# Attention with a mixture layer on one core: local probabilities transposed by a DMA from a float16 pair in SBUF

## Chip, cores, metric

The kernel runs on one core of a Trainium2 chip (trn2). The metric is the device time of one execution in microseconds; before the change the median of three runs is 1051.26 us (1050.98 to 1051.85).

## What is computed

Two attentions over the same q, k, v are added, and the sum goes through a gated layer:

```python
batch, n_heads, seq, head_dim = (8, 8, 576, 64)
q_d, k_d, v_d = means of q, k, v over 4 neighbours      # 144 rows
out_up = repeat(softmax(scale * q_d @ k_d.T) @ v_d, 4)
mask = abs(pos[:, None] - pos[None, :]) < 4
out_local = softmax(where(mask, scale * q @ k.T, -1e9)) @ v
x = (out_up + out_local)                                # 4608 x 512
gate = 1 / (1 + exp(-(x @ w_gate))); val = x @ w_val    # 512 x 1536
return (gate * val) @ w_out                             # 1536 x 512
```

All arrays are float32.

## The kernel before

**Units.** The 64 pairs of batch and head are worked in 32 units of two heads; four units make a batch of 576 tokens. The local attention of a unit is cut into ten blocks of 58 queries, each with its window of 64 keys. Their scores and probabilities lie in one tile `t` of 128 x 640 f32: two blocks share the 128 partitions, five such pairs lie side by side.

**Steps of a unit.** `unit_steps` returns them by name. `s0` and `s1` make the scores (`s_local`, line 475) and `s1` also the exponentials; `sm` (`p2b`, line 500) divides by the sums, for most units on GpSimd, line 507. `a0` and `a1` (`t_local`, line 559) transpose `t`, three blocks of 128 x 128 and then two, on TensorE against the identity into a PSUM tile `at` (line 563), and `parts_of` (line 554) takes it to SBUF as `at16`. For units 0 to 5 (`plain`, NPLAIN = 6) that is one f32 tile. For units 6 to 31 it is a pair of float16 tiles: ScalarE casts the high part (line 555), VectorE subtracts it from the f32 value for the low part (line 557). `x` (`av_local`, line 590) multiplies `at16` with the values `vblk`: ten blocks of three products each (high with high, high with low, low with high; `product`, line 416), then adds the down-sampled output `od` (line 607) and takes the sum apart for the next layer. `d0`, `d1`, `dn`, `at`, `od` do the down-sampled attention with its own small transposes (`adt`, line 573).

**Pools.** `wk` holds `t` and `at16` with two buffers each. PSUM has five banks `mm` and three banks `att`; from unit 4 on the tiles of scores, of both transposes and of `od` share the three.

**The gated layer.** Batches 0 and 1 multiply directly (`moe_gate`, `moe_val`). From batch 2 on `pair` works on two 2x2 blocks at once in seven products (tiles `pg_b_p_..` and `pv_b_p_..`) whose sums VectorE, ScalarE and GpSimd make (lines 811 to 825); twelve pairs a batch, then `act` and `low` leave the product of gate and value as a float16 pair in `gq` (lines 848 and 853). Their weights come from DRAM through a ring of three slots (`wring`, line 782). Then `out_group` and `out_evict` multiply by the output weights: tiles `po_b_m_h`, evicted at lines 729 and 731, stored at line 733.

**Order of the work.** A table of step positions `T` says where each step of each unit stands (`at`, line 886); the units of a batch are worked while the batch before it is in the gated layer. `add` collects the steps, and they are issued in the order of their positions; a scheduler then sets the order on each engine. All DMAs are issued from SP, in order: an issue that waits holds back those behind it.

Of the kernel before, what the change touches and what calls it, by code (L numbers as in the profile page):

```python
# [9 lines left out]
F16 = mybir.dt.float16  # L10
# [9 lines left out]
P = 128  # L20
# [5 lines left out]
R = 58  # L26
WIN = 64
NBLK = 10
NJ = NBLK // 2
# [16 lines left out]
NPLAIN = 6  # L46
# [18 lines left out]
def attention_moe(ctx, tc, qk, qkd, v, vd, wg, wv, wo, mask, out):  # L65
    nc = tc.nc
# [369 lines left out]
    def unit_steps(u):  # L436
# [120 lines left out]
                nc.vector.tensor_tensor(out=dst[1], in0=src, in1=dst[0], op=ALU.subtract)  # L557

        def t_local(j0, j1):
            n = j1 - j0  # L560
            pt = att(f"at_{u}_{j0}")
            for j in range(j0, j1):
                nc.tensor.transpose(pt[:, (j - j0) * P : (j - j0 + 1) * P], s["t"][:, j, :], ident)  # L563
            if j0 == 0:
                s["at"] = in_parts(wk.tile([P, 2, NBLK, R], F16, tag="at", name=f"at16_{u}"), NBLK)
            parts_of([x[:, 2 * j0 : 2 * j1, :] for x in s["at"]], pt[:, : n * P].rearrange("p (g r) -> p g r", r=64)[:, :, :R])

        def t_down():
            mine(ad, u)
# [20 lines left out]
        def av_local(i0, i1):  # L590
            mine(VT, u)
            pt = mm(f"x_{u}_{i0}")
            for i in range(i0, i1):
                product(pt[:, (i - i0) * R : (i - i0 + 1) * R], [x[:, i] for x in VBp], [x[:, i] for x in s["at"]])
            if i0 == 0:
                s["xs"] = xs2 if b >= 2 and u % 2 else xs1
                assert b < 2 or all(("a", k, i) in done for k in "gvo" for i in range(NPC))
                own(s["xs"], u)
            t0, t1 = i0 * R, min(i1 * R, S)
            g0, g1 = t0 // 4, t1 // 4  # L600
            o = s["xs"][:, t0:t1].rearrange("p (g f) -> p g f", f=4)
            x = pt[:, : t1 - t0].rearrange("p (g f) -> p g f", f=4)
            y = s["od"][:, g0:g1].unsqueeze(2).to_broadcast([P, g1 - g0, 4])
            if NPAIR <= u < NPLAIN:
                nc.vector.scalar_tensor_tensor(out=o, in0=x, scalar=sxb[:, b : b + 1], in1=y, op0=ALU.mult, op1=ALU.add)
            else:
                nc.vector.tensor_tensor(out=o, in0=x, in1=y, op=ALU.add)
# [276 lines left out]
        return T["O0"] + T["OD"] * m if b == 0 else start(b) + (TP * (84 + 10.5 * m) / 126 if b < 2 else TB * (72 + 11 * m) / 116)  # L884

    def at(u, k):
        b, hp = divmod(u, NPAIR)
        if b == 0:
            return T[f"p{u}{k}"]
        if b == 1:  # L890
            return T[f"b{u}"] + T["q" + k]
        return start(b) + T[f"m{hp}{k}"] * span(b - 1) / 118
# [178 lines left out]
```

## Time and profile before

| | |
|---|---|
| median of three runs | 1051.26 us (1050.98 to 1051.85) |
| span of the profiled execution | 1051.7 us |
| TensorE | 1018.7 us busy, 97% |
| VectorE | 747.2 us, 71% |
| GpSimd | 556.4 us, 53% |
| ScalarE | 475.6 us, 45% |
| DMA queue of SP | 45.6% of 16 engines, 167.5 MB |

The span of the profiled execution is the time from its first to its last instruction; the profile gives no other time for this execution, and 1051.7 lies inside the spread of the three runs. In the rows further down PE is TensorE, PEld its weight loads, DVE VectorE, ACT ScalarE, POOL GpSimd, SPq SP's queue. A timeline merges neighbouring instructions of one line and shape (x30), and the time beside the start is what they cover. A matmul's record ends where its modelled end lies, so records overlap.

### The profile page before, as it was taken

The numbers are of one execution on the slowest core, as the hardware profiler recorded it, in microseconds if no ns is written. First come the engines' busy times: TensorE is split into PE (matmuls) and PEld (weight loads), VectorE is DVE, ScalarE is ACT, GpSimd is POOL, SyncE is SP. The second block draws the span as 40 slices with busy tenths as digits, with TensorE's granted clock in tenths as the row PEclk, the third lists the DMA queues.
The fourth block names the chain that finished last, engine by engine and source line by source line (L and its number), as shares of the span: only waits on it lengthen the run. The fifth ranks groups of instructions, "written<-read, shape, count | busy, mean of one in ns | idle before, by whom it ended". The sixth has DMA issues, their size and how long they took to land.

```text
span 1051.7 us, 23801 instructions
## 1 busy us (share of the span) xinstructions
PE 1018.7 (97%) x9587; PEld 810.7 (77%) x9587; DVE 747.2 (71%) x1417; ACT 475.6 (45%) x1064; POOL 556.4 (53%) x579
## 2 busy tenths in 40 slices
PE   8998989999889999999999999999999999999998
PEld 6776667777677877887778777887778877887776
DVE  6989999587896778746885578746886478825640
ACT  4868757334443444524553344434454344522320
POOL 7435368343564558644783548644783548612320
PEclk9999999999999999999999999999999999999999
DMA  9447943423434357344654347344563355313501
GB/s 360 162 160 254 349 164 125 136 85 113 166 124 172 126 178 253 116 147 143 236 190 142 123 165 264 119 147 140 204 225 112 125 183 191 120 35 119 178 33 46
DMA packets 53245, 169.01 MB, mean 161 GB/s; under 512 B 12560, under 2 KB 18832, under 8 KB 53136
## 3 DMA queue, kind: packets, MB, share of 16 engines
q1 hardware_dynamic: 53136, 167.50, 45.6%
q8 instruction: 75, 1.23, 0.5%
q14 instruction: 34, 0.28, 0.1%
HBM read 147.03 MB, written 20.45 MB: 159 GB/s over the span
## 4 chain that ended last, share of the span: by engine, by line
PE 69%; DVE 17%; ACT 4%; issue 4%; POOL 3%; DMA 3%; SPq 0%; DVEq 0%; ACTq 0%; POOLq 0%
PE po L420 26%; PE pv L420 16%; PE pg L420 16%; PE s L420 3%; PE x L420 2%; PE sd L420 2%; PE od L420 2%; DMA arena<-in_wo_dram 1%; DVE tanh L702 1%; DVE wo L192 1%; PE at L563 1%; DVE gq L192 1%; DVE arena L811 1%; PE adt L573 1%; DVE vblk L192 1%
## 5 line engine op out<-in xcount | busy, mean ns | idle before, releaser
L420 PEld LDWEIGHTS <-arena 128*128 128x128 f16 x4176 | 403.8, 98 | 119.1 <-issue 5.1
L420 PE MATMUL po<-gq,wo 128*128 128x288 f16 x2304 | 295.2, 288 | 5.1 <-ACT gq L191 2.8
L420 PE MATMUL pg<-arena 128*128 128x288 f16 x2088 | 278.4, 287 | 3.7 <-DVE tanh L702 1.5
L420 PE MATMUL pv<-arena 128*128 128x288 f16 x2088 | 277.0, 287 | 1.6 <-ACT arena L294 0.8
L420 PEld LDWEIGHTS <-wo 128*128 128x128 f16 x2304 | 225.2, 98 | 63.4 <-issue 4.0
L811 POOL TENSOR_TENSOR arena<-arena 128x288 f32<-128x288 f32 x126 | 127.7, 1018 | 108.3 <-ACT arena L825 61.0
L811 DVE TENSOR_TENSOR arena<-pv,arena 128x288 f32<-128x288 f32 x180 | 80.6, 453 | 50.5 <-PE pv L420 38.6
L729 DVE TENSOR_SCALAR arena<-po,osc 128x288 f32<-128x288 f32 x32 | 16.5, 515 | 81.6 <-PE po L420 81.4
L548 POOL TENSOR_TENSOR ad<-e,sme 72x288 f32<-72x288 f32 x54 | 52.8, 997 | 21.7 <-DVE sme L539 15.6
L192 DVE SCALAR_TENSOR_TENSOR vblk<-v,svb,vblk 64x640 f16<-64x640 f32 x52 | 57.5, 1106 | 8.7 <-ACT vblk L191 7.3
L191 ACT ACTIVATE vblk<-v,svb 64x640 f16<-64x640 f32 x52 | 42.9, 825 | 38.7 <-PE x L420 20.4
L811 DVE TENSOR_TENSOR arena<-pg,arena 128x288 f32<-128x288 f32 x126 | 54.5, 447 | 5.9 <-PE pg L420 3.9
L497 POOL TENSOR_TENSOR t<-t,mx 128x640 f32<-128x640 f32 x32 | 40.2, 1258 | 33.2 <-DVE mx L496 24.7
L409 POOL TENSOR_TENSOR vd<-vd 128x384 f32<-128x384 f32 x29 | 25.5, 879 | 53.6 <-DMA vd<-in_vd_dram 53.2
L420 PEld LDWEIGHTS s<-qk 64*64 64x64 f32 x1200 | 42.5, 134 | 14.7 <-issue 11.1
L420 PE MATMUL s<-qk 64*64 64x64 f32 x1200 | 52.2, 224 | 0.0
L507 POOL TENSOR_TENSOR t<-t,sm 128x640 f32<-128x640 f32 x24 | 35.7, 1486 | 27.1 <-DVE sm L505 21.9
L420 PE MATMUL sd<-kdblk,qks 128*72 128x288 f32 x128 | 43.1, 420 | 6.4 <-ACT e L531 3.3
L531 ACT ACTIVATE e<-sd,mxd 72x144 f32<-72x144 f32 x128 | 47.1, 371 | 1.9
L819 ACT COPY arena<-pg 128x288 f32<-128x288 f32 x36 | 14.3, 397 | 74.2 <-PE pg L420 74.1
L295 POOL TENSOR_TENSOR arena<-arena 128x512 f16<-128x512 f32 x24 | 32.0, 1353 | 29.0 <-ACT arena L294 28.9
L409 POOL TENSOR_TENSOR qkd<-qkd 128x576 f32<-128x576 f32 x29 | 35.5, 1224 | 18.7 <-DMA qkd<-in_qkd_dram 18.7
(147 smaller groups left out, 1557.1 us busy)
## 6 DMA issues: line engine op xcount, KB each, us to landing
arena<-wd SPq DMA_DIRECT2D x72, 896.0 KB, 4.7
qk<-in_qk_dram SPq DMA_DIRECT2D x30, 610.0 KB, 5.6
qkd<-in_qkd_dram SPq DMA_DIRECT2D x29, 576.0 KB, 3.7
vd<-in_vd_dram SPq DMA_DIRECT2D x29, 384.0 KB, 4.3
v<-in_v_dram SPq DMA_DIRECT2D x32, 320.0 KB, 5.1
arena<-in_wg_dram SPq DMA_DIRECT2D x12, 512.0 KB, 4.1
arena<-in_wv_dram SPq DMA_DIRECT2D x12, 512.0 KB, 4.9
arena<-in_wo_dram SPq DMA_DIRECT2D x12, 512.0 KB, 5.7
```

What stands on the lines that cost most here:

```text
L191: nc.scalar.activation(hi, src, AF.Copy, scale=sc)
L192: return nc.vector.scalar_tensor_tensor(out=lo, in0=src, scalar=sc, in1=hi, op0=ALU.mult, op1=ALU.subtract)
L295: nc.gpsimd.tensor_tensor(out=lo, in0=a, in1=hi, op=ALU.subtract)
L409: nc.gpsimd.tensor_tensor(out=x[:, :, 0:2], in0=x[:, :, 0:2], in1=x[:, :, 2:4], op=ALU.add)
L420: nc.tensor.matmul(o, w[a], x[c], start=first and i == 0, stop=last and i == len(pairs) - 1)
L497: nc.gpsimd.tensor_tensor(out=t, in0=t, in1=mx.unsqueeze(2).to_broadcast([P, NBLK, WIN]), op=ALU.subtract)
L507: eng.tensor_tensor(out=t, in0=t, in1=sm.unsqueeze(2).to_broadcast([P, NBLK, WIN]), op=ALU.mult)
L531: nc.scalar.activation(s["e"][:, qb, h, :], pt[:QM, h * SD : (h + 1) * SD], AF.Exp, bias=mx[:, h : h + 1], scale=QKSCALE / 16, accum_out=s ...
L548: eng.tensor_tensor(out=AD[:, qb].rearrange("p c h k -> p h c k")[:, :, :, :KC], in0=s["e"][:, qb].rearrange("p h (c k) -> p h c k", c=NKC ...
L729: nc.vector.tensor_scalar(out=dst_, in0=pt[:, :HN], scalar1=sc, scalar2=None, op0=ALU.mult)
L811: eng.tensor_tensor(out=dst_, in0=x, in1=y, op=ALU.add)
L819: nc.scalar.copy(sx[:, 0], go(P1))
```

## The change

For units 6 to 31 `a0` no longer uses TensorE. ScalarE casts `t` into the first half of a new SBUF tile `hl` (128 x 2 x 640 f16), VectorE puts the rest into the second, and one DMA transpose on SP takes all ten blocks of 128 x 128 to `at16`, whose rows are now 64 wide instead of 58. `a1` does nothing for these units. `at16` and `hl` have one buffer each (the plain units alternate between the two). Since one buffer can't be written while the unit before still reads it, `at` places `a0` and `a1` of a unit behind `x` of the unit before; the old `at` is now called `placed`.

```diff
--- before.py
+++ after.py
@@ -557,13 +557,21 @@
                 nc.vector.tensor_tensor(out=dst[1], in0=src, in1=dst[0], op=ALU.subtract)
 
         def t_local(j0, j1):
+            if j0 == 0:
+                s["at16"] = wk.tile([P, 2, NBLK, WIN], F16, tag="hl" if plain and u % 2 else "at", name=f"at16_{u}", bufs=1)
+                s["at"] = in_parts(s["at16"], NBLK)
+            if not plain:
+                if j0 == 0:
+                    t = s["t"].rearrange("p j c -> p (j c)")
+                    hl = wk.tile([P, 2, NJ * 2 * WIN], F16, tag="hl", name=f"hl_{u}", bufs=1)
+                    parts_of([hl[:, 0], hl[:, 1]], t)
+                    nc.sync.dma_start_transpose(s["at16"].rearrange("p t a b -> p (t a b)").rearrange("p (j r) -> p j r", r=P), hl.rearrange("p t c -> p (t c)"))
+                return
             n = j1 - j0
             pt = att(f"at_{u}_{j0}")
             for j in range(j0, j1):
                 nc.tensor.transpose(pt[:, (j - j0) * P : (j - j0 + 1) * P], s["t"][:, j, :], ident)
-            if j0 == 0:
-                s["at"] = in_parts(wk.tile([P, 2, NBLK, R], F16, tag="at", name=f"at16_{u}"), NBLK)
-            parts_of([x[:, 2 * j0 : 2 * j1, :] for x in s["at"]], pt[:, : n * P].rearrange("p (g r) -> p g r", r=64)[:, :, :R])
+            parts_of([x[:, 2 * j0 : 2 * j1, :R] for x in s["at"]], pt[:, : n * P].rearrange("p (g r) -> p g r", r=64)[:, :, :R])
 
         def t_down():
             mine(ad, u)
@@ -591,7 +599,7 @@
             mine(VT, u)
             pt = mm(f"x_{u}_{i0}")
             for i in range(i0, i1):
-                product(pt[:, (i - i0) * R : (i - i0 + 1) * R], [x[:, i] for x in VBp], [x[:, i] for x in s["at"]])
+                product(pt[:, (i - i0) * R : (i - i0 + 1) * R], [x[:, i] for x in VBp], [x[:, i, :R] for x in s["at"]])
             if i0 == 0:
                 s["xs"] = xs2 if b >= 2 and u % 2 else xs1
                 assert b < 2 or all(("a", k, i) in done for k in "gvo" for i in range(NPC))
@@ -884,6 +892,10 @@
         return T["O0"] + T["OD"] * m if b == 0 else start(b) + (TP * (84 + 10.5 * m) / 126 if b < 2 else TB * (72 + 11 * m) / 116)
 
     def at(u, k):
+        p = placed(u, k)
+        return max(p, placed(u - 1, "x") + (0.05 if k == "a0" else 0.1)) if k in ("a0", "a1") and u >= NPLAIN else p
+
+    def placed(u, k):
         b, hp = divmod(u, NPAIR)
         if b == 0:
             return T[f"p{u}{k}"]
```

Where instructions stand. TensorE, end of the pair products of batch 2 and start of its output (names: `pg_2_5_..` and `pv_2_5_..` the last pairs' products, `at_14_0` and `at_14_3` the two PSUM tiles of unit 14's transposes, `adt_14` the small transposes, `x_13_0` the product of unit 13, `sd_15_1` scores of unit 15). Before:

```order
L420 MATMUL pg_2_5_26_5487<-arena_109 128x288
L563 MATMUL at_14_0_5505<-ident_103,t_14_5110 128x128
L420 MATMUL pv_2_5_00_5496<-arena_109 128x288
...
L563 MATMUL at_14_0_5505<-ident_103,t_14_5110 128x128 x2
L573 MATMUL adt_14_5612<-ident_103,ad_127 128x72 x6
L563 MATMUL at_14_3_5659<-ident_103,t_14_5110 128x128
L420 MATMUL x_13_0_5516<-at16_13_5190,vblk_129 128x58
...
L563 MATMUL at_14_3_5659<-ident_103,t_14_5110 128x128
L420 MATMUL sd_15_1_5695<-kdblk1_125,qks_15_5286 72x288
...
L563 MATMUL at_15_0_5776<-ident_103,t_15_5389 128x128 x3
L420 MATMUL po_2_0_0_5623<-gq_111,wo16_110 128x288
```

and with the change:

```order
L420 MATMUL pg_2_5_26_5431<-arena_109 128x288
L581 MATMUL adt_14_5554<-ident_103,ad_127 128x72 x3
L420 MATMUL pv_2_5_00_5440<-arena_109 128x288
...
L581 MATMUL adt_14_5554<-ident_103,ad_127 128x72 x3
L420 MATMUL sd_15_1_5632<-kdblk1_125,qks_15_5230 72x288
L420 MATMUL x_13_0_5453<-at16_13_5137,vblk_129 128x58
...
L420 MATMUL x_14_8_5702<-at16_14_5494,vblk_129 128x58
...
L420 MATMUL po_2_0_0_5565<-gq_111,wo16_110 128x288
```

The ten transposes of units 14 and 15 are gone from between the products; the small transposes, `sd_15_1` and `od_14` (not shown) stand a few places earlier, the rest keeps its neighbours.

ScalarE at the same place (`pv_2_5_55` a product of the last pair, `at16_14` the unit's transposed probabilities, line 848 or 856 the scaling into `gq` of the last pair). Before:

```order
L611 CAST arena_109<-arena_109 128x2x288
L825 COPY arena_109<-pv_2_5_55_5565 128x288
L555 CAST at16_14_5509<-at_14_3_5659 128x232
L611 CAST arena_109<-arena_109 128x4x288
L529 ACTIVATE mxd_15_1_5697<-mxd_15_1_5697 72x2
L531 ACTIVATE e_15_5450,sme_15_5451<-sd_15_1_5695,mxd_15_1_5697 72x144 x2
L848 ACTIVATE gq_111<-arena_109 128x2x576
```

and with the change:

```order
L619 CAST arena_109<-arena_109 128x2x288
L531 ACTIVATE e_15_5394,sme_15_5395<-sd_15_1_5632,mxd_15_1_5634 72x144 x2
L833 COPY arena_109<-pv_2_5_55_5507 128x288
L555 CAST hl_15_5714<-t_15_5333 128x640
L595 ACTIVATE od16_14_5643<-od_14_5639,sxb_140 128x144
L619 CAST arena_109<-arena_109 128x4x288
L856 ACTIVATE gq_111<-arena_109 128x2x576
```

The cast of unit 14's second part is gone from there, and the cast of unit 15 into `hl`, which must wait until the transpose of unit 14 has read that buffer, stands ahead of the scaling into `gq`.

SP at the same place (line 782 or 790 loads of pair weights, `v18` and `v19` values of batch 4, line 733 or 741 stores of the output). Before:

```order
L782 DMA arena_109<-wd_116 128x3584 x3
L205 DMA v18_5912<-in_v_dram 128x640
L782 DMA arena_109<-wd_116 128x3584
L205 DMA v19_5929<-in_v_dram 128x640
L733 DMA out_dram<-arena_109 128x384
L733 DMA out_dram<-arena_109 128x192
```

and with the change:

```order
L790 DMA arena_109<-wd_116 128x3584 x4
L568 DMA_TRANSPOSE at16_14_5494<-hl_14_5495 128x10x128
L205 DMA v18_5842<-in_v_dram 128x640
L790 DMA arena_109<-wd_116 128x3584
L568 DMA_TRANSPOSE at16_15_5713<-hl_15_5714 128x10x128
L741 DMA out_dram<-arena_109 128x192
L741 DMA out_dram<-arena_109 128x384
```

Two transposes came in, one behind the weight loads and ahead of `v18`, one behind the next weight load and ahead of the stores.

## Rows read from the trace of the kernel before

**Rows 1.** The page, part 1: busy us, share of the span, instructions.
```profile
PE 1018.7 (97%) x9587; PEld 810.7 (77%) x9587; DVE 747.2 (71%) x1417; ACT 475.6 (45%) x1064; POOL 556.4 (53%) x579
```

**Rows 2.** The page, part 4: shares of the chain by engine and by line.
```profile
PE 69%; DVE 17%; ACT 4%; issue 4%; POOL 3%; DMA 3%; SPq 0%; DVEq 0%; ACTq 0%; POOLq 0%
PE po L420 26%; PE pv L420 16%; PE pg L420 16%; PE s L420 3%; PE x L420 2%; PE sd L420 2%; PE od L420 2%; DMA arena<-in_wo_dram 1%; DVE tanh L702 1%; DVE wo L192 1%; PE at L563 1%; DVE gq L192 1%; DVE arena L811 1%; PE adt L573 1%; DVE vblk L192 1%
```

**Rows 3.** Stretches: length, then busy us (instructions) of each engine, PEclk, DMA, GB/s.
```profile
186.00:341.00 155.00, 146.30 (x1388) 116.19 (x1389) 116.84 (x201) 64.34 (x146) 75.93 (x68) 0.98 0.38 135
341.00:461.00 120.00, 120.00 (x1168) 96.11 (x1167) 87.38 (x165) 52.64 (x116) 72.44 (x76) 1.00 0.50 172
...
821.00:941.00 120.00, 119.53 (x1163) 95.63 (x1161) 80.71 (x155) 51.43 (x114) 64.18 (x66) 1.00 0.37 130
```

**Rows 4.** Tile at: duration ns min/median/max, first and last start, forms.
```profile
L563 PE MATMUL at<-ident,t x160: 270/273/330, 21.8 to 931.7; 128*128 128x128 f32 x160
L555 ACT CAST at<-at x52: 337/402/455, 182.8 to 932.2; 128x348 f16<-128x348 f32 x26, 128x232 f16<-128x232 f32 x26
L557 DVE TENSOR_TENSOR at<-at,at x52: 383/453/522, 187.1 to 932.6; 128x348 f16<-128x348 f32 x26, 128x232 f16<-128x232 f32 x26
```

**Rows 5.** TensorE's timeline, pairs of the fourth batch: start us, us, what.
```profile
520.73 0.71 PE L563 MATMUL at<-ident,t 128*128 128x128 f32 x5
521.28 3.84 PE L420 MATMUL pv<-arena 128*128 128x288 f16 x30
```

**Rows 6.** TensorE's timeline, end of the pairs and output of the third batch.
```profile
426.84 0.98 PE L420 MATMUL x<-at,vblk 128*128 128x58 f16 x30
...
444.42 0.98 PE L420 MATMUL x<-at,vblk 128*128 128x58 f16 x30
445.23 0.53 PE L563 MATMUL at<-ident,t 128*128 128x128 f32 x3
445.60 2.37 PE L420 MATMUL po<-gq,wo 128*128 128x288 f16 x18
```

**Rows 7.** ScalarE's timeline at the same place.
```profile
431.25 0.67 ACT L611 CAST arena<-arena 128x576 f16<-128x576 f32 x1
431.83 0.39 ACT L825 COPY arena<-pv 128x288 f32<-128x288 f32 x1
```

**Rows 8.** VectorE's timeline at the same place.
```profile
433.38 0.76 DVE L612 TENSOR_TENSOR arena<-arena 128x576 f16<-128x576 f32 x1
434.06 0.39 DVE L557 TENSOR_TENSOR at<-at,at 128x232 f16<-128x232 f32 x1
...
440.41 1.36 DVE L853 SCALAR_TENSOR_TENSOR gq<-arena,gq 128x1152 f16<-128x1152 f32 x1 [1.23 <-ACT gq L848]
```

**Rows 9.** DMA issues: what, count, KB each, median us from issue to landing.
```profile
v<-in_v_dram SPq DMA_DIRECT2D x32, 320.0 KB, 5.1
...
out_dram<-arena SPq DMA_DIRECT2D x8, 256.0 KB, 2.1
...
wd<-arena SPq DMA_DIRECT2D x12, 128.0 KB, 3.8
...
gq<-in_vd_dram SPq DMA_DIRECT2D x3, 384.0 KB, 11.5
```

**Rows 10.** SP's timeline at the place of groups 6 to 8.
```profile
432.89 0.33 SPq L205 DMA_DIRECT2D v<-in_v_dram  x1
...
448.66 0.33 SPq L205 DMA_DIRECT2D v<-in_v_dram  x1
```

**Rows 11.** Line 507 on VectorE: duration ns min/median/max, first and last start.
```profile
L507 DVE TENSOR_TENSOR t<-t,sm x8: 792/814/1927, 19.9 to 278.7; 128x640 f32<-128x640 f32 x8
```

**Rows 12.** TensorE's timeline around the products x of units 6 and 7.
```profile
192.75 0.97 PE L420 MATMUL x<-at,vblk 128*128 128x58 f16 x30
...
204.23 0.98 PE L420 MATMUL x<-at,vblk 128*128 128x58 f16 x30
```

## The prediction

> **What bounds the kernel now.** I read the engines' totals first, then the stretches, then the chain, and only then the operations that the change touches. TensorE shows 97% busy and VectorE 71% [rows 1]. A busy TensorE proves little, since its records overlap, so the second look is at the stretches: between 341 and 461 us TensorE shows 120.0 of 120 us at a granted clock of 1.00, while VectorE has 33 us to spare; the four stretches of 120 us after it show 119.5 to 119.9, the last of them 119.53. Only between 186 and 341 us does it fall to 146 of 155 us [rows 3]. The chain of waits says the same: 69% TensorE, and the transposes that the change removes (line 563) stand on it with 1% [rows 2], some 10 us. So from the second batch on TensorE sets the pace, and time taken off it is time gained, unless something new makes it wait.
>
> **What is removed.** Units 6 to 31 lose five f32 transposes each, 26 x 5 = 130. One record lasts 273 ns [rows 4], but that is from its start to its modelled end, and the next begins before it. What one takes from the stream is the step between starts: five start at 520.73 us and the next matmul at 521.28, so 0.55 us for five, 0.11 each [rows 5]; three start at 445.23 us, the next matmul at 445.60, 0.12 each [rows 6]. So 26 x 0.55 = **14.3 us** of TensorE. I take half where another engine ends the waits: units 8 to 11, in the stretch that ends at 341 us and is not full [rows 3], and units 13, 17, 21, 25 and 29, whose five stand among the pair products, where VectorE's share of the chain lies [rows 2, 5]. 9 x 0.275 = 2.5 us less: **11.8 us**. The Trainium skill ("TensorE: Matmul & The Clock Gate", Part 4: PE-mode transpose) gives some 275 ns for a transpose in a kernel's context. The records of 273 ns agree with it, but by it the sum would be 130 x 0.275 = 35.8 us, and the steps between starts speak against that.
>
> **What ScalarE and VectorE do instead.** Removed are 52 casts from PSUM of 0.40 us and 52 subtractions of 0.45 us, both mean over the two sizes [rows 4]. Added are 26 casts of 128x640 from SBUF, and 26 subtractions. Nearest rows: a cast of 128x576 took 0.67 us [rows 7], so 0.74 for 640; a subtraction of 128x576 took 0.76 us [rows 8], so 0.85. Per unit ScalarE goes from 0.80 to 0.74 us and VectorE from 0.91 to 0.85: nothing. The new subtraction reads both operands from SBUF, and a VectorE operation of that kind and size varies from 0.79 to 1.93 us [rows 11], while the old one, with an operand in PSUM, stayed near its mean. At worst that is 1.1 us a unit on an engine with 33 us free per batch; it costs only where VectorE is short, and is part of the first rival. PSUM: the three attention banks serve two tiles fewer per unit, which can only help.
>
> **What is added: the DMA.** 26 transposes of 128x1280 f16, 320 KB read and written in SBUF. The trace of before shows none, so its time from issue to landing, call it D, is bounded by other transfers. From below: a 256 KB store landed in 2.1 us. From above: 384 KB loads into an almost full queue took 11.5 us. Between them: 320 KB loads took 5.1 us, and a store of 128 KB that is cut into 512 pieces of 256 bytes took 3.8 us [rows 9]. If the pieces set the pace, 1280 of them would take 9.5. I take **6 us**, nearest the load of the same size, with something for the pieces.
>
> What must wait for it? Two things, and both follow from there being one buffer of each kind. First, the product `x` of the same unit. The transpose of unit u may not start before `x` of unit u-1 has read the buffer. In a batch the tight pairs are the third and fourth unit: `x` of unit 13 ends at 427.82 us and `x` of unit 14 starts at 444.42 [rows 6], 16.6 us apart, and the next pair likewise. Units 6 and 7 are 10.5 us apart [rows 12]. D = 6 fits everywhere; the first two units of a batch lie further apart.
>
> Second, the cast into `hl` of the next unit, which overwrites what the transpose reads. The order shows where it hurts: the cast of unit 15 stands on ScalarE just behind the copy of `pv_2_5_55`, and ahead of the scaling of `gq` for the last pair. Issued when `x` of unit 13 ends, the transpose of unit 14 lands at 427.82 + D. Behind that come the cast (0.74), the subtraction (0.85) and what now lies between the old subtraction's end, 434.45 us, and the end of the last `gq`, 441.77 [rows 8], 7.32 us. `gq` is wanted when the next `po` starts, at 445.60 [rows 6]. So 427.82 + D + 8.91 must not pass 445.60: **D up to 8.9 us costs nothing**. The copy ahead of it ends at 432.22 [rows 7], so at D = 6 ScalarE stands still for 1.6 us, and this slack covers it; without it those 1.6 us would be lost in each of six places.
>
> The SP queue runs in order, and each transpose waits there with everything behind it. Behind that of unit 14 stands the `v` load issued at 432.89 us now, 5.1 us after `x` of unit 13; behind that of unit 15 an output store and a `v` load, at 448.66 now, 3.4 us after `x` of unit 14 [rows 6, 10]. The issue itself may be longer than the 0.33 us of a plain one; up to 3.4 us is covered, and then weight loads three slots ahead still have room. Nothing.
>
> The moved step (`a0` of u behind `x` of u-1) shifts the third unit of each batch by a place or two in the table of steps, and unit 7 by 8.7 of its steps; it adds no engine work.
>
> **The sum.** 1051.7 - 11.8 = 1039.9 us for the profiled span, which is 0.4 us above the median of the runs (1051.26) and inside their spread. From the median: **1039.5 us**. With all 14.3 us and some relief of PSUM it is 1035 to 1037.
>
> **Rivals.**
> *Partial gain.* If VectorE or GpSimd sets the pace among the pair products, because the new subtractions are slowed by SBUF traffic, only transposes that stood among the `po` or at the end of the pairs pay: two units per batch in five batches, and units 6, 7 and 11, 13 x 0.55 = 7.2 us, **1044 us**. For it: the chain has VectorE with 17% [rows 2]. Against it: 33 us of free VectorE time per batch [rows 3]. 15%.
>
> *Slower: the transpose lands late.* Above 8.9 us each further microsecond is lost in six places (units 11, 15, 19, 23, 27 and 31, by the cast on ScalarE) and above 10.5 also at unit 7. 6 x (D - 8.9) + (D - 10.5) reaches 11.8 at D = 10.8: that is the point from which it decides. At the upper bound, 11.5, it is 16.6 us lost, **1056 us**. For it: no transposing DMA is in the trace, the pieces are small, and the bound of 9.5 by pieces is already past the slack. Against it: the stores and loads of this size. 23%. The Trainium skill ("VectorE: DVE Perf Modes", The three transpose paths) has 1309 ns for one 128x128 block by DMA; an estimate of ten such blocks one after another is 13.1 us, and by it the sum would be 27.8 us lost, 1067 us. The same skill ("Advanced Engine Details and Errata", X-Bar Transpose) calls transposing DMAs as fast as regular ones, which is the forecast. No run yet shows which.
>
> *Much more.* If the 273 ns were truly lost per transpose, 35.5 us, 1016 us. The steps between starts exclude it nearly: 2%.
>
> *No change* (8%): the late landing and the gain cancel, D near 10.8. That the change does not do what it says is closed by the order: 26 transposes stand on SP, and TensorE has none from unit 6 on.
>
> **Chances and range.** 0.2% of the time, 2.1 us, is about what a measurement of this kernel can tell from no change. Forecast (1034 to 1043) 52%, partial gain 15%, much more 2%: faster 0.69. Same 0.08. Slower 0.23. The range takes in the forecast, the partial gain, no change and the slower case to a little past the upper bound of D: 1034 to 1058 us; left out are the far late landing and the much larger gain. The likeliest case's own range is 1034 to 1043.
>
> **What would show it.** Right: no `at` matmul after unit 5, TensorE at 120 of 120 us in shorter batches, batches of 120 us some 2 us shorter; DMA transposes landing within 9 us; `po` behind `x` of the third unit without a gap. Wrong: TensorE idle before `x` or the following `po`, released by a DMA or by `gq`; ScalarE waiting for a DMA at the cast of line 555 longer than some 4 us; SP held for more than 3 us by a single transpose, with weight loads late.

## The result and the profile after

The changed kernel takes 1060.49 us (median of four runs, 1059.53 to 1062.43) beside 1051.12 for the kernel before (four runs, 1049.87 to 1051.85). The ratio is 1.0096, 95% interval 1.0072 to 1.0119: 9.4 us **slower**, where 11.8 us faster was forecast. The time lies outside the range given, 1034 to 1058.

The page of the changed kernel, part 1 and the first line of part 4 (compare [rows 1, 2]):

```profile
PE 1014.5 (96%) x9457; PEld 796.4 (75%) x9457; DVE 759.9 (72%) x1391; ACT 473.8 (45%) x1038; POOL 555.9 (53%) x579
...
PE 65%; DVE 18%; DMA 5%; ACT 4%; POOL 4%; issue 3%; SPq 0%; POOLq 0%; DVEq 0%; ACTq 0%
```

TensorE is busy 4 us less, but its share of the chain falls from 69 to 65%, and DMA rises from 3 to 5%. So waits have come onto the path. The stretches tell where (length, then busy us and instructions of PE, PEld, DVE, ACT, POOL; PEclk, DMA, GB/s). The kernel before, in a stretch that [rows 3] does not have by itself:

```profile
341.00:396.00 55.00, 55.00 (x554) 43.55 (x553) 41.65 (x84) 24.18 (x54) 31.41 (x32) 1.00 0.45 156
```

and the changed kernel:

```profile
186.00:341.00 155.00, 143.05 (x1354) 112.68 (x1353) 110.83 (x189) 62.89 (x137) 71.55 (x65) 0.97 0.43 141
341.00:396.00 55.00, 50.43 (x488) 38.49 (x488) 41.09 (x78) 22.99 (x51) 27.03 (x31) 0.97 0.44 149
588.00:708.00 120.00, 119.53 (x1145) 93.65 (x1144) 86.06 (x156) 50.91 (x110) 70.70 (x76) 1.00 0.55 180
```

Between 341 and 396 us TensorE was full before, and now stands still for 4.6 of 55 us. In a later stretch, 588 to 708 us, it is busy 119.5 of 120 us, where it was 119.9 before.

Where it went is read from the starts of `x` on TensorE's timeline, which mark the units. Unit 19 to 23 of the kernel before, starts at 582.39 and then

```profile
626.65 0.98 PE L420 MATMUL x<-at,vblk 128*128 128x58 f16 x30
...
701.74 0.98 PE L420 MATMUL x<-at,vblk 128*128 128x58 f16 x30
```

and of the changed kernel, from 588.57:

```profile
633.62 0.96 PE L420 MATMUL x<-at,vblk 128*128 128x58 f16 x30
...
708.10 0.96 PE L420 MATMUL x<-at,vblk 128*128 128x58 f16 x30
```

That is 119.35 us a batch before and 119.53 now: the batches did not get shorter at all. The whole difference of the two profiled executions (spans 1051.7 and 1057.7) splits so:

| from | before | after | difference |
|---|---|---|---|
| start to `x` of unit 4 | 154.05 | 153.99 | -0.06 |
| `x` of unit 4 to unit 11 | 189.20 | 188.90 | -0.30 |
| **unit 11 to unit 12** | 44.16 | 51.23 | **+7.07** |
| unit 12 to 28, four batches | 478.34 | 478.80 | +0.46 |
| unit 28 to the end | 185.93 | 184.83 | -1.10 |

The rest of the 9.4 us is the choice of executions: the device time of the changed kernel's profiled run, 1059.53, is its span plus 1.8 us, and so it was in all later runs. By that the profiled execution of the kernel before took some 1053.5 us (an estimate), above its median, and that of the changed kernel lies below its own. There are two questions, then: what costs 7 us once, and what eats 2.3 us in every batch.

**The one-time loss.** Ahead of unit 12 the kernel makes the sums of the pair weights in twelve steps (function `sums`): GpSimd adds, VectorE takes sums, ScalarE casts, VectorE subtracts, SP stores; GpSimd's next step waits for that store. In the tenth step VectorE did this in the kernel before (line 771 is the subtraction of the sums, 607 the addition of `x` of unit 10, 192 the value parts of unit 11):

```profile
324.95 1.23 DVE L771 TENSOR_TENSOR arena<-arena 128x1024 f16<-128x1024 f32 x1 [0.73 <-ACT arena L770]
326.09 0.82 DVE L607 TENSOR_TENSOR xs<-x,od 128x464 f32<-128x464 f32 x2
326.82 2.21 DVE L192 SCALAR_TENSOR_TENSOR vblk<-v,svb,vblk 64x640 f16<-64x640 f32 x2
```

and does this now (the same as lines 779, 615 and 192):

```profile
324.90 0.81 DVE L615 TENSOR_TENSOR xs<-x,od 128x464 f32<-128x464 f32 x2
325.63 2.21 DVE L192 SCALAR_TENSOR_TENSOR vblk<-v,svb,vblk 64x640 f16<-64x640 f32 x2
327.87 1.23 DVE L779 TENSOR_TENSOR arena<-arena 128x1024 f16<-128x1024 f32 x1
```

The order of three operations has changed; none of them belongs to the transposes. SP's queue shows what follows, before:

```profile
326.20 0.33 SPq L772 DMA_DIRECT2D wd<-arena  x1
329.06 0.34 SPq L205 DMA_DIRECT2D v<-in_v_dram  x1
329.45 0.42 SPq L205 DMA_DIRECT2D vd<-in_vd_dram  x1
329.92 0.43 SPq L205 DMA_DIRECT2D qk<-in_qk_dram  x1
```

and after:

```profile
327.87 0.34 SPq L205 DMA_DIRECT2D v<-in_v_dram  x1
328.26 0.42 SPq L205 DMA_DIRECT2D vd<-in_vd_dram  x1
328.73 0.43 SPq L205 DMA_DIRECT2D qk<-in_qk_dram  x1
329.26 1.22 SPq L780 DMA_DIRECT2D wd<-arena  x1
```

The value parts free the buffer of `v`, so its load and the two behind it go out first, and the store `wd` follows them. The chain of the changed kernel has its price:

```profile
327.87 1.23 DVE arena L779
...
329.26 7.48 DMA wd<-arena
...
336.90 2.13 POOL arena L766
```

The store lands 7.48 us after its issue. Before, it landed in 3.1 us (issued at 326.20, GpSimd went on at 329.5). The last store of the sums leaves at 357.6 in place of 347.0. After it VectorE has a softmax and the scale of a batch's values to do, which TensorE waits for up to 363.6.

TensorE's waits between 341 and 396 us make 4.6 of the 7 us. A part of the rest is its clock, granted at 1.00 for this stretch in the kernel before. In the changed kernel TensorE stood still for 4.6 of 23 us, and behind that its granted clock was at the lower of its two levels, 1.2 GHz, for most of four microseconds:

```profile
341.00:364.00 23.00, 18.43 (x196) 14.50 (x195) 15.88 (x27) 7.05 (x13) 10.37 (x12) 1.00 0.28 100
364.00:368.00 4.00, 4.00 (x20) 2.55 (x21) 2.90 (x13) 1.66 (x10) 2.65 (x4) 0.57 0.92 224
```

A mean of 0.57 over 4 us makes some 1.7 us lost (an estimate). So a wait can cost more than its own length.

**The steady loss.** Adding up the steps from one matmul's start to the next over units 19 to 23, by tile, gives: `at` 2.32 us before, none now; `s` 6.85 before, 8.14 now; `pv` 31.28 and 32.38; `pg` 31.20 and 31.41; all others within 0.1. So the price of a transpose, 0.11 to 0.12 us [rows 5, 6], came off in full, and scores and pair products took it back. For the scores the timeline shows why. The scheduler cut them into more pieces (a group here is a run of score products between other products): 87 groups in the program from unit 12 on, in place of 55, and between 470 and 950 us of the trace 67 in place of 43, six more a batch. Three of the changed kernel:

```profile
659.60 0.56 PE L420 MATMUL s<-qk 64*64 64x64 f32 x12
660.44 1.63 PE L420 MATMUL pv<-arena 128*128 128x288 f16 x12 [0.28 <-DVE tanh L819]
662.00 0.56 PE L420 MATMUL s<-qk 64*64 64x64 f32 x12
662.50 2.38 PE L420 MATMUL pv<-arena 128*128 128x288 f16 x18
664.81 0.32 PE L420 MATMUL s<-qk 64*64 64x64 f32 x2
665.07 0.91 PE L420 MATMUL pv<-arena 128*128 128x288 f16 x6
```

Twelve score products (64x64 f32) take 0.50 us up to the next start, two take 0.26. That is 0.024 us each and 0.21 us for a group as such; six groups make 1.26 us, and 1.29 is what `s` lost. The Trainium skill ("TensorEngine Tiling (Array Packing)", Key Properties) says that a change of the tiling mode drains TensorE. The rows, where 64x64 tiles follow 128x128 ones, agree in that such a change takes time; they do not show what happens in it. The pair products pay as well. From the start of one to the next start is 0.122 us where another pair product follows, and 0.216 us where a score group does, in both kernels. Over these four units 15 score groups follow a pair product in place of 7, which makes 0.75 of the 1.31 us that `pv` and `pg` lost. Waits for VectorE are the other part; one of them, 0.28 us, stands in the second row.

The new subtraction itself is on VectorE (tile `hl`, ns min/median/max):

```profile
L555 ACT CAST hl<-t x26: 708/726/732, 176.4 to 918.5; 128x640 f16<-128x640 f32 x26
L557 DVE TENSOR_TENSOR hl<-t,hl x26: 783/1008/2129, 179.8 to 920.3; 128x640 f16<-128x640 f32 x26
L568 SPq DMA_TRANSPOSE at<-hl x26: 1258/1346/2260, 180.7 to 930.9; - x26
```

1.01 us in the middle and up to 2.13, where 0.85 was estimated. It depends on what GpSimd does. At 718.84 GpSimd stood still, at 775.30 it was already at work, and at 441.64 it started just behind VectorE:

```profile
441.64 0.78 DVE L557 TENSOR_TENSOR hl<-t,hl 128x640 f16<-128x640 f32 x1
...
718.84 0.82 DVE L557 TENSOR_TENSOR hl<-t,hl 128x640 f16<-128x640 f32 x1 [2.19 <-ACT hl L555]
...
775.30 2.13 DVE L557 TENSOR_TENSOR hl<-t,hl 128x640 f16<-128x640 f32 x1
```

and GpSimd:

```profile
441.71 1.38 POOL L819 TENSOR_TENSOR arena<-arena 128x288 f32<-128x288 f32 x1 [0.46 <-DVE sme L539]
...
774.86 1.14 POOL L409 TENSOR_TENSOR qkd<-qkd 128x576 f32<-128x576 f32 x1
775.96 0.78 POOL L819 TENSOR_TENSOR arena<-arena 128x288 f32<-128x288 f32 x1
776.71 2.67 POOL L411 TENSOR_TENSOR kdblk<-qkd 64x144 f32<-64x144 f32 x2
```

In the six units where GpSimd was idle throughout, the subtraction took 0.79 to 0.83 us. In the four where a GpSimd instruction started during it, it took 0.78 to 0.82. In the other sixteen a GpSimd instruction was already running when it started, and it took 0.96 to 2.13. So VectorE was held up in this trace only where GpSimd had started first; at 441.71, where VectorE had, GpSimd's instruction took 1.38 us, and one of the same line and shape took 0.78 at 775.96. The Trainium skill ("SBUF — State Buffer", Who interferes with whom) says that a VectorE instruction with two inputs in SBUF contends with a GpSimd instruction that reads SBUF. That agrees. The old subtraction, which had one input in PSUM, stayed between 0.38 and 0.52 us for its two sizes [rows 4].

### The profile page after: what moved, and what is told of

The parts are those of the page before. It is cut to its first block, busy times and chain, and to the rows that moved or that the text cites. A ratio compares the mean times of both kernels' runs of the same rounds, so it can differ in the third digit from the quotient of the medians.

```text
span 1057.7 us, 23536 instructions
## 1 busy us (share of the span) xinstructions
PE 1014.5 (96%) x9457; PEld 796.4 (75%) x9457; DVE 759.9 (72%) x1391; ACT 473.8 (45%) x1038; POOL 555.9 (53%) x579
## 2 busy tenths in 40 slices
DMA packets 87357, 177.52 MB, mean 168 GB/s; under 512 B 46672, under 2 KB 52944, under 8 KB 87248
## 4 chain that ended last, share of the span: by engine, by line
PE 65%; DVE 18%; DMA 5%; ACT 4%; POOL 4%; issue 3%; SPq 0%; POOLq 0%; DVEq 0%; ACTq 0%
PE po L420 22%; PE pv L420 17%; PE pg L420 16%; PE s L420 3%; PE sd L420 2%; DVE arena L775 2%; DMA wd<-arena 2%; PE x L420 2%; PE od L420 2%; POOL arena L766 1%; DVE gq L192 1%; DMA v<-in_v_dram 1%; DVE arena L779 1%; DVE wo L192 1%; DVE vblk L192 1%
## 5 line engine op out<-in xcount | busy, mean ns | idle before, releaser
L420 PE MATMUL pv<-arena 128*128 128x288 f16 x2088 | 282.4, 288 | 3.4 <-DVE arena L819 1.1
L497 POOL TENSOR_TENSOR t<-t,mx 128x640 f32<-128x640 f32 x32 | 44.0, 1374 | 43.3 <-DVE mx L496 33.8
L420 PEld LDWEIGHTS s<-qk 64*64 64x64 f32 x1200 | 46.0, 134 | 21.8 <-issue 19.1
L420 PE MATMUL s<-qk 64*64 64x64 f32 x1200 | 60.1, 225 | 0.0
L548 POOL TENSOR_TENSOR ad<-e,sme 72x288 f32<-72x288 f32 x54 | 43.2, 818 | 21.9 <-DVE sme L539 13.3
L409 POOL TENSOR_TENSOR qkd<-qkd 128x576 f32<-128x576 f32 x29 | 39.4, 1359 | 27.2 <-DMA qkd<-in_qkd_dram 24.6
L739 ACT ACTIVATE arena<-po,osc 128x288 f32<-128x288 f32 x32 | 15.4, 497 | 73.6 <-PE po L420 73.5
```

Source lines behind the costliest of these rows:

```text
L409: nc.gpsimd.tensor_tensor(out=x[:, :, 0:2], in0=x[:, :, 0:2], in1=x[:, :, 2:4], op=ALU.add)
L420: nc.tensor.matmul(o, w[a], x[c], start=first and i == 0, stop=last and i == len(pairs) - 1)
L497: nc.gpsimd.tensor_tensor(out=t, in0=t, in1=mx.unsqueeze(2).to_broadcast([P, NBLK, WIN]), op=ALU.subtract)
L548: eng.tensor_tensor(out=AD[:, qb].rearrange("p c h k -> p h c k")[:, :, :, :KC], in0=s["e"][:, qb].rearrange("p h (c k) -> p h c k", c=NKC ...
L739: nc.scalar.activation(dst_, pt[:, :HN], AF.Copy, scale=sc)
```

## Experiments

**Theory A:** both losses come from the order that the scheduler makes once the transposes are gone, once among the sums, and in each batch as pieces of scores. **Rivals:** B, the traffic of the DMA transposes; C, the shifted steps and single buffers; D, VectorE's subtraction from SBUF bounds the pair products. All twelve runs, each beside the kernel before on the same chip, whose median there was 1048.5 to 1049.9 us. "Period" is the mean of the four batches from `x` of unit 12 to 28:

| run | us | ratio (95%) | unit 11 to 12 | period |
|---|---|---|---|---|
| before (first profile) | | | 44.16 | 119.6 |
| changed (first profile) | 1060.5 | 1.0096 (1.0072 to 1.0119) | 51.23 | 119.7 |
| steps only | 1048.2 | 0.9989 (0.9972 to 1.0007) | 44.15 | 119.3 |
| DMA from unit 16 | 1051.4 | 1.0015 (0.9998 to 1.0032) | 44.15 | 119.8 |
| TensorE held | 1055.4 | 1.0063 (1.0042 to 1.0084) | 50.33 | 118.2 |
| all held | 1049.7 | 1.0025 (1.0006 to 1.0045) | 43.92 | 119.6 |
| all held to 352 us | 1045.6 | 0.9959 (0.9943 to 0.9976) | 45.45 | 118.0 |
| VectorE held to 352 us | 1046.0 | 0.9962 (0.9943 to 0.9980) | 47.63 | 117.9 |
| scores joined | 1054.6 | 1.0042 (1.0021 to 1.0063) | 54.81 | 118.1 |
| before, scores joined | 1067.1 | 1.0163 (1.0131 to 1.0196) | 51.55 | 121.9 |
| sums first | 1054.2 | 1.0050 (1.0034 to 1.0067) | 46.53 | 119.7 |
| TensorE held, sums first | 1049.5 | 1.0000 (0.9982 to 1.0018) | 45.32 | 118.2 |
| TensorE held, low part on GpSimd | 1049.4 | 0.9998 (0.9983 to 1.0013) | 45.13 | 117.5 |
| combined | 1040.9 | 0.9921 (0.9893 to 0.9949) | 43.61 | 117.7 |

In the expectations of the first six runs the groups of `x` in the trace are counted, where unit 5 stands as two, so their "unit 12 to unit 13" is the column "unit 11 to 12".

**Steps only.** All units transposed on TensorE, the rest of the change kept.

```diff
-                s["at16"] = wk.tile([P, 2, NBLK, WIN], F16, tag="hl" if plain and u % 2 else "at", name=f"at16_{u}", bufs=1)
+                s["at16"] = wk.tile([P, 2, NBLK, WIN], F16, tag="hl" if u % 2 else "at", name=f"at16_{u}", bufs=1)
...
-            if not plain:
+            if False:
```

> The changed table of steps, the rows of 64 and the single alternating buffers stay, but every unit is transposed on TensorE as before. Theory A (the loss of 9.4 us needs the DMA path: about 7 us once, in the stage of the weight sums between 343 and 394 us, and in each later batch a gain of 2.3 us on TensorE that new pieces of the score products and waits on VectorE eat up): with TensorE's transposes back both go, 1051 us, 1049 to 1054. Rival C (the single buffers and the later steps cost the time by themselves, whatever engine transposes): 1058 us or more, with units 12 on some 7 us later than in the kernel before.

Measured 1048.2, ratio 0.9989, and 44.15 us from unit 11 to 12. The later steps cost nothing. The single buffers are not tested here: with TensorE's transposes `at16` alternates between the two, so that a unit never writes the buffer that the unit before it reads, as in the kernel before. That half of C falls with the run "all held to 352 us" further down, which keeps every single buffer of the change and is faster than the kernel before.

**DMA from unit 16.**

```diff
+NDMA = 16
...
-            if not plain:
+            if u >= NDMA:
```

Units 6 to 15 also keep their old places in the table of steps and the two alternating buffers (not shown).

> The DMA path only for units 16 to 31, units 6 to 15 on TensorE. Theory A: the one-time loss of 7 us falls in the stage of the weight sums, which ends ahead of unit 12, so it goes; the later batches keep their period of 119.4 to 119.8 us: 1051 us, 1049 to 1053. Rival B (the transposes' traffic or SP's held queue costs something at every unit, 9.4 us over 26): 16 of 26 units remain, 5.8 us, so 1057 us.

Ratio 1.0015, against 1.0055 that B would give. The loss at the sums is gone (44.15), and the batches with DMA transposes have the old period, 119.8. So the 7 us belong to the stage of the sums, and the steady batches gain nothing by the change as it stands.

**TensorE held.** A list of the order in the kernel before, made into edges of order without waits (cut from the function that reads the list):

```diff
...
+        for x, y in zip(order, order[1:]):
+            tc.add_manual_dep(pe[y], pe[x].name, mybir.DependencyInfo(mybir.DependencyClass.NoSync, mybir.DependencyReason.DATA), reason="pinned")
```

> The changed kernel with TensorE's instructions held in the order they have in the kernel before (without the removed transposes); the other engines' order is left to the scheduler. Theory A: the score products stand in 11 groups a batch again and not in 17, 6 x 0.19 us = 1.1 us a batch come back in five batches, so the period of units 14, 18, 22 is 118.2 to 119.0 us; the loss at the weight sums may stay, since it lies on other engines: 1050 to 1056 us. Rival D (VectorE with its low parts from SBUF is the bound among the pair products): the period stays at 119.5 and the time at 1060. Rival B: 1058 to 1062.

Periods of 117.9 to 118.4 us: theory A's number. The scores are back at 6.70 us a batch, and VectorE's subtraction at a median of 0.83 us: in 17 of the 26 units no GpSimd instruction was running when it started, in place of 10. The sums still lose (50.33), so that is not TensorE's order. D in its strong form falls, but from unit 20 to 21 it takes 39.74 us where 39.56 less 0.55 for the five transposes is 39.01: something is still missing there.

**All held.** The same for four engines; a unit's cast and subtraction stand where its first cast and first subtraction stood before.

```diff
+        for e, text in ORDERS.items():
...
+            for x, y in zip(order, order[1:]):
+                tc.add_manual_dep(seq[y], seq[x].name, mybir.DependencyInfo(mybir.DependencyClass.NoSync, mybir.DependencyReason.DATA), reason="pinned")
```

> The changed kernel with the order of TensorE, VectorE, ScalarE and GpSimd held as in the kernel before; the cast and the subtraction of a unit stand where its first cast and subtraction stood. Theory A in its strong form (the scheduler's new order is all of the loss): 1040 to 1046 us, periods of 118 us and no gap of TensorE at 355 to 364 us. Theory A with stores that land late behind loads and transposes: the gap at 355 to 364 us stays, 1047 to 1053 us. Rival B (traffic) or D (VectorE's low parts): periods of 119.5 us or more, 1055 us or more.

Half right. The sums are whole again (43.92) with every DMA transpose in place, which speaks against B a second time. But the periods are 119.1 to 120.3, so the old order of the other three engines seems a bad one for the new work further on: in a batch TensorE waits 0.5 us for VectorE ahead of `x`, and again ahead of `po`. Why VectorE is late at these two was not followed further; the next run, which holds that order only until the sums are done, has short periods again.

**All held to 352 us, VectorE held to 352 us.** TensorE held throughout, the others only until the sums are done. The edit is shown against the run before; the second run lists VectorE alone.

```diff
+PINNED = {'DVE': 543, 'Activation': 379, 'Pool': 177}
...
-            for x, y in zip(order, order[1:]):
+            n = PINNED.get(e, len(order))
+            for x, y in list(zip(order[:n], order[1:n])) + [(order[n - 1], y) for y in order[n:]]:
```

> As the run with TensorE's order held throughout, and VectorE, ScalarE and GpSimd held to the order of the kernel before only up to 352 us of its trace (that is past the weight sums); from there on the scheduler is free on these three. Theory A (the loss at the weight sums is the scheduler's new order on the three engines, not the transposes' traffic): x of unit 12 to x of unit 13 takes 44 us as in the run with all four held (43.92), and the periods of the later batches are the 118.0 to 118.4 us of the run with TensorE held alone; together some 6 us less than before: a ratio of 0.993 to 0.996, about 1043 to 1045 beside 1049.4. Rival E (what all four held gained at the sums comes back as a wait later, because the later order stands on the earlier): periods of 119 us or more, ratio of 0.999 or more.

> As the run before this one, but of the three engines only VectorE is held up to 352 us; ScalarE and GpSimd are free. It tells which order makes the loss at the weight sums. If VectorE's order does (its 1.0 us subtraction and the value casts put ahead of the sums, on the engine that stands in the chain there): x of unit 12 to x of unit 13 in 44 to 45 us, ratio 0.993 to 0.997. If it is ScalarE's or GpSimd's order, or stores that land late behind loads and transposes whatever the order is: 49 to 51 us, ratio 1.003 to 1.007.

Ratios 0.9959 and 0.9962, periods of 117.6 to 118.4: **faster than before**, with all 26 DMA transposes. The step from unit 11 to 12 takes 45.45 us, with VectorE alone held 47.63. A part of the loss lies ahead of unit 11, so the fuller count is from unit 4 to unit 12: 242.0 us with only TensorE held, 233.2 with VectorE held too, 231.2 with all. VectorE's order makes most of the loss, the others some 2 us of it. Rival E falls.

**Scores joined, in the changed kernel and, as a control, in the kernel before.**

```diff
-            for g in range(2 * j0, 2 * j1):
...
+            with tc.high_priority(offset=1500):
+                for g in range(2 * j0, 2 * j1):
...
```

> The changed kernel with one edit: the products of the scores have priority, so that TensorE does them in 29 groups (units 12 to 31) in place of 87; nothing is held. Theory A (each step into and out of a group of scores takes 0.19 us): some 11 groups a batch less, 2.1 us, so periods of 117.4 to 118.4 us against 119.7; the loss at the sums stays: ratio 0.998 to 1.002. Rival D (VectorE is the bound among the pairs, the pieces fill time that is lost anyway): periods of 119.5, ratio 1.008 to 1.010.

> The control: the same edit in the kernel before the change, whose scores then stand in 30 groups in place of 55 (units 12 to 31). By 0.19 us a group it gains 5 x 0.19 = 1.0 us a batch: periods of 118.4 to 118.8 us against 119.6, ratio 0.994 to 0.997. If the pieces are no cost of their own: 119.4 to 119.8, ratio 0.999 to 1.001.

In the changed kernel the period fell to 118.1 us as expected (116.1 to 119.9 by batch); the sums lost more (54.81), so the ratio missed. The control missed outright: 1.6% slower. Its scores did become cheaper, 5.64 us a batch in place of 6.85, but the priority moved their places, and TensorE then stood still, twice in a batch for 1.5 us, behind VectorE's sums of the pair products. A piece has its price, and yet fewer pieces are no gain when they stand where another engine is late. Priority was the wrong tool: it changes more than the pieces.

**Sums first.** Only the three operations of the tenth step are put back.

```diff
+    for i in later["x", 10] + later["v", 11]:
+        tc.add_manual_dep(i, zlow[9].name, mybir.DependencyInfo(mybir.DependencyClass.NoSync, mybir.DependencyReason.DATA), reason="sums first")
```

> The changed kernel with one thing held: on VectorE, the last subtraction of the tenth step of the weight sums stands ahead of the additions of x of unit 10 and of the value parts of unit 11, as it does in the kernel before; nothing else is held. Theory A, narrowed (this one exchange on VectorE sends the store of that step to SP 3 us later, behind three loads that VectorE's work set free, where it takes 7.5 us to land and not 2.8, so the next step of the sums starts 7 us later): the store stands ahead of the loads and lands in about 2.8 us, x of unit 11 to x of unit 12 (groups 12 and 13 of x in the trace, where unit 5 has two) takes 44 to 47 us in place of 51.2, 4 to 7 us come back: 1.002 to 1.005 of the time before. Rival F (no single place: many small delays of the sums add up): 50 to 51 us there, ratio 1.008 to 1.010.

```profile
327.76 0.33 SPq L782 DMA_DIRECT2D wd<-arena  x1
330.62 0.34 SPq L205 DMA_DIRECT2D v<-in_v_dram  x1
```

The store (first line) goes out ahead of the loads, GpSimd goes on at 332.22, 4.5 us later and not 7.6, and 4.7 of the 7 us come back: 46.53 us, ratio 1.0050. The store itself landed in 4.3 us, not in the 2.8 expected. The trace points to ScalarE for the rest: its cast for this step stands behind the two value casts (323.74, 1.66 us), and VectorE stood still for 2.8 us ahead of the subtraction. No run puts that back by itself. One exchange of neighbours thus cost some 5 us, half of the loss; rival F falls.

**TensorE held, sums first.** The edits of the runs "TensorE held" and "sums first" together:

```diff
...
+    pinned([i for i in nc.cur_bb.bb.instructions if type(i).__name__ == "InstMatmult"])
...
+    for i in later["x", 10] + later["v", 11]:
...
```

> The same exchange held, and TensorE's order as in the kernel before throughout. If the two causes are separate and add up: periods of 118.0 to 118.4 us as with TensorE's order alone, and x of unit 11 to x of unit 12 in 44 to 47 us in place of 50.3: ratio 0.996 to 1.000. If VectorE's order in the sums is wrong in more places than this one: 48 to 50 us there, ratio 1.002 to 1.006.

45.32 us and 118.2: the causes are separate and add up; ratio 1.0000, at the upper end of what was expected. From unit 4 to unit 12 the exchange gives back 6.8 us here (242.0 to 235.2) and 3.6 us with TensorE's order free (240.1 to 236.5), so "some 5 us" is a middle value.

**Low part on GpSimd.** TensorE held, and

```diff
-                    parts_of([hl[:, 0], hl[:, 1]], t)
+                    nc.scalar.copy(hl[:, 0], t)
+                    nc.gpsimd.tensor_tensor(out=hl[:, 1], in0=t, in1=hl[:, 0], op=ALU.subtract)
```

> TensorE's order as in the kernel before throughout, and the low part of the split made by GpSimd in place of VectorE, in all 26 units. Rival D (the 0.8 to 1.4 us of VectorE for a low part are what is missing among the pair products, 39.7 us from x of unit 20 to x of unit 21 where 39.0 was due): that stretch takes 39.0 to 39.3 us and the periods 117.3 to 117.8. Theory A (VectorE is not the bound, order is): 39.6 to 39.8 and periods of 118.0 to 118.4, or longer where GpSimd's 1.3 us delay the transpose. The loss at the sums stays in both, ratio 1.003 to 1.007.

```profile
629.72 0.96 PE L421 MATMUL x<-at,vblk 128*128 128x58 f16 x30
...
668.53 0.96 PE L421 MATMUL x<-at,vblk 128*128 128x58 f16 x30
```

38.81 us from unit 20 to 21, and periods of 117.4 to 117.8: relieving VectorE gives back the part that was missing, though GpSimd takes 1.40 us for it. That the subtraction itself was what was missing, as D says, is not shown by this alone. The run "VectorE held to 352 us" has the same stretch at 39.03 us, with all 26 subtractions still on VectorE:

```profile
626.41 0.96 PE L425 MATMUL x<-at,vblk 128*128 128x58 f16 x30
...
665.43 0.96 PE L425 MATMUL x<-at,vblk 128*128 128x58 f16 x30
```

Its periods are 117.9 us on average (117.6 to 118.2 by batch). So of the 0.7 us a batch from 118.2 to 117.5 some 0.4 can stand for the subtraction; the other 0.3 came off by another order alone.

The loss at the sums did not go, as the 45.13 us of the table suggest; it lies ahead of unit 11. Unit 4 to unit 11 takes 195.5 us, in place of 191.7 with TensorE held and 189.2 before, and unit 4 to unit 12 takes 240.6, beside 242.0 and 233.4. GpSimd works for the sums there, which may be why the loss moved; this run does not separate it.

**Combined.** All held to 352 us, TensorE throughout, low part on GpSimd from unit 12 on. The edit is shown against the run "all held to 352 us".

```diff
-                r.append(nc.vector.tensor_tensor(out=dst[1], in0=src, in1=dst[0], op=ALU.subtract).ins)
+                r.append((nc.gpsimd if u >= 12 else nc.vector).tensor_tensor(out=dst[1], in0=src, in1=dst[0], op=ALU.subtract).ins)
```

> The three findings together: TensorE's order as in the kernel before throughout, VectorE, ScalarE and GpSimd held to their earlier order up to 352 us, and from unit 12 on the low part of the split on GpSimd. If they add up, x of unit 11 to x of unit 12 takes 44 to 46 us, the periods are the 117.3 to 117.8 us of the run with all low parts on GpSimd, and the time is 0.5 us a batch, 2 to 3 us in all, below that of the run with all engines held up to 352 us (1045.6 beside 1049.9): ratio 0.992 to 0.995. That would be the gain that the prediction gave to this change, 11.8 us, up to 3 or 4 us. If GpSimd's slower low part brings a new wait: periods of 118 us, ratio 0.996 or more.

```profile
PE 1001.7 (97%) x9457; PEld 793.6 (77%) x9457; DVE 741.1 (71%) x1371; ACT 476.6 (46%) x1038; POOL 582.0 (56%) x599
341.00:396.00 55.00, 55.00 (x511) 42.67 (x510) 44.46 (x86) 26.16 (x57) 35.42 (x36) 1.00 0.59 187
```

1040.9 beside 1048.5 us, ratio 0.9921 (0.9893 to 0.9949): 8 us faster than the kernel before, and 1.7% below the changed kernel by the two ratios. TensorE is full between 341 and 396 again, and has lost 17 us of busy time against [rows 1]. Its profiled span is 3.4 us below that of the run "all held to 352 us"; 1.5 of these lie in the four batches from unit 12 to 28, one of which took 118.5 us and not the 117.3 to 117.8 expected.

## Why the prediction was wrong

**What bounds the kernel:** right in the main. TensorE sets the pace from the second batch on, but with so little room that each wait for VectorE counts.

**What is removed:** right in size. The 0.11 us step was the true price of a transpose: 2.32 us a batch went out of TensorE's stream. The half counts for units among the pairs were too careful for TensorE itself. With TensorE's order held and VectorE relieved the periods fell by 2.0 us, between the 1.9 a batch that the half counts make and the full 2.3.

**The DMA:** its time to landing, D in the prediction, was 3.4 us (3.3 to 5.1), not 6, and far from the threshold of 8.9. The small pieces did not set the pace, by which it would have been 9.5, although they are there (the packets under 512 bytes rose from 12560 to 46672):

```profile
DMA to landing us min/median/max: 3.3/3.4/5.1
```

The slower rival, a transpose that lands late, did not happen; the casts into `hl` waited for a DMA 1.9 us in all. SP was held for 1.35 us at a time, 2.26 at most, inside the 3.4 allowed (3.3, counted to the end of unit 14's last product [rows 6, 10]). Between the two sentences of the Trainium skill that the prediction cites, the measurement decides. The 1309 ns for one block ("VectorE: DVE Perf Modes", The three transpose paths) do not multiply: the estimate of 13.1 us for ten is four times what they took here. That transposing DMAs are as fast as regular ones ("Advanced Engine Details and Errata", X-Bar Transpose) agrees, with loads of `v`, the same size but from DRAM, at 5.1 us [rows 9].

**The step that failed** is one that the sum makes without a term: that the order on the engines stays. I took TensorE's stream of before, less 130 transposes, and left all else in place, as the section on the change says ("the rest keeps its neighbours"). None of the rivals has a new order in it. The order had been compared at the end of the pairs of one batch, where it held. It was not compared where another engine than TensorE ends the waits: at the weight sums, although [rows 3] showed that stretch not full. There three operations changed their order and 7 us were lost, some 5 of them by that exchange. And in the batches 32 more groups of scores and the waits beside them ate the 2.3 us.

**"Nothing" for VectorE** was the second error. The mechanism of the first rival, new subtractions slowed in SBUF among the pair products, was real, but no rival had it together with a new order. The 33 us of VectorE that are free in a batch [rows 3] were no argument: they are not free where TensorE waits for it. Its share was the smaller one. It was 0.7 us a batch at most (118.2 to 117.5), of which 0.3 also came off without moving the subtraction, against 1.5 us from TensorE's order (119.7 to 118.2).

To set the profiled span of before "inside the spread" of the runs was wrong: with the 1.8 us around it, its time was some 1053.5 us, above all of them. The forecast started from the median and is not touched by it.

## What to carry to other kernels

When a scheduler sets the order, an edit on one engine is an edit on all of them: compare the new order first at the stage where the bound engine is not full, for there, as at the sums here, an exchange of neighbours can decide when a store leaves, what it queues behind, and so when the next step starts. Before a change that takes work off the bound engine is given up, run it once with the old order held; here that turned 9 us lost into 4 gained, and with the low part on GpSimd as well into 8. Count a subtraction that moves from PSUM to SBUF at its worst behind a running GpSimd instruction, not at its mean.

## Not expected of the hardware

A DMA transpose of ten 128x128 float16 blocks in high and low parts (320 KB) lands in 3.4 us, and holds SP's queue for 1.35 us, four plain issues. A group of 64x64 f32 products costs 0.21 us beside its products, and 0.09 us more at the product ahead of it. A 512 KB store took 7.5 us behind three loads, 3.1 us ahead of them in the kernel before and 4.3 in the run "sums first". The same subtraction took 0.78 to 0.83 us where no GpSimd instruction was running at its start, and up to 2.13 where one was. What was not tried: the price of more transposing traffic by itself, and the order of ScalarE alone among the sums.
